# Filter products, butterflies and gate products in fewer, longer VectorE operations, with a new order and a choice of engines

## The chip, the cores and the metric

The kernel runs on one core of a Trainium2 chip. The metric is device time in microseconds: the time of one execution on the device, where the median of several executions is taken. The kernel before takes 239.01 us (three runs, 238.78 to 239.78). The profiled execution has a span of 235.4 us from its first to its last instruction; all times within the kernel are counted from the start of that span.

Five engines matter. TensorE (PE) multiplies matrices, with PEld its weight loads. VectorE (DVE) and ScalarE (ACT) do elementwise work and move results out of PSUM. GpSimd (POOL) issues the loads of q, k, v and the weights, and SyncE (SP) issues the outputs and the transposes by DMA.

## The reference

There are 8 batches, 8 heads, 576 positions and 64 values per head. A linear attention (cosformer) is followed by a gated long convolution (Hyena):

```python
# attention: theta = pi/2 * pos / S
phi(x) = concat(relu(x) * cos(theta), relu(x) * sin(theta))        # 64 -> 128
kv  = einsum('bhsf,bhsd->bhfd', phi(k), v);  z = phi(k).sum(s)
att = einsum('bhsf,bhfd->bhsd', phi(q), kv) / (einsum(phi(q), z) + 1e-6)
x   = att with the heads side by side                               # (8, 576, 512)

# gated convolution
x1, x2, x3 = split(x @ w_proj)                                      # 512 -> 3 * 512
x2_conv = irfft(rfft(x2, axis=1) * rfft(filter, axis=0), n=576)     # along the sequence
out = (x1 * x2_conv * x3) @ w_out
```

## The kernel before

Names in the profile are those of the tiles here. The plan is a list of words: each word runs one more piece of a step (up to its next `yield`), in program order, and every engine takes its own instructions in that order. `'v` behind a word sends an eviction to VectorE instead of ScalarE, `'a` sends a product to ScalarE instead of VectorE, `'b` moves a transposed q in one piece. `~` holds a load back until the last VectorE operation and the last transpose before it in the plan have finished. The first number of a word is the batch; the rest is a channel group, a pair of heads or a part.

```python
def ev(out, in_, mul=None):                  # an eviction: VectorE with 'v, else ScalarE
    ...

def step_pk(b, half):                        # kp: relu(k) * cos, relu(k) * sin
    for j in range(NJ):
        for x, col in enumerate((ccol, scol)):
            if which[0] == "a":
                nc.scalar.activation(out=dst, in_=src, func=AF.Relu, scale=c)
            else:
                tsc(dst, src, c, AL.mult, 0.0, AL.max)
            yield
# step_pq (qp) is alike: relu(q), and relu(q) * tcol for each of five columns
# step_va: v into va, with a column of ones;  step_kv: the matmuls kv<-va,kp
# step_qt: q transposed, on TensorE for batches 0 and 1, by DMA from batch 2 (qpt<-qp)
# step_num: matmuls num<-kvs,qpt, then rcp and att = num * rcp on VectorE
# step_fx: matmuls that fold att along the sequence, and an eviction to fx
# step_xt: att transposed by DMA into xt (batches 1 to 7);  step_xp: on TensorE, batch 0

def step_x2(b, bl):                          # "pr": x2 = fx @ w_proj[x2], evicted to x2f
    ...

def step_dft(b, bl):                         # bl 0, 1: 512 wide; bl 2: 128 wide
    ...                                      # matmuls dft<-x2f,fcos and dft<-x2f,fsin
    yield
    xf = work.tile([128, 2, n], FP16, tag=f"xf{n}", bufs=2)
    ev(xf, u[:, :, 0:n])
    yield
    h = (hE, hO, hL)[bl]
    tt(out=m1, in0=xf, in1=hr, op=AL.mult)
    yield
    tt(out=m2, in0=xf, in1=h[:, 0] broadcast, op=AL.mult)
    yield
    tt(out=yf[:, 0], in0=m1[:, 0], in1=m2[:, 1], op=AL.subtract)
    yield
    tt(out=yf[:, 1], in0=m1[:, 1], in1=m2[:, 0], op=AL.add)
    yield

def step_gate(w):                            # "ga": w = 0 (x1), "gb": w = 2 (x3)
    def gate(b, c):                          # c: one of four groups of 128 channels
        u = unit(f"x{w}_{b}_{c}")
        for i in range(NC):
            for hf in range(2):
                nc.tensor.matmul(u[:, hf, 0:HS], wp16[:, i, ...], xt[:, i, ...], ...)
        yield
        x = work.tile([128, 2, HS], FP16, tag=f"x{w}s", bufs=2)
        ev(x, u[:, :, 0:HS])                 # x0s or x2s
        yield

def step_g(b, c):                            # g = x1 * x3
    tt(out=g[:, c], in0=x0s, in1=x2s, op=AL.mult)
    yield

def step_inv(b, c):                          # six matmuls inv<-itab,yf and inv<-itl,yf
    ...                                      # from all three yf
    yield
    eq = tile([128, 2, 2, QS], FP16, tag="eq", bufs=4)
    ev(eq, u[:, :, 0:HS])
    yield

def step_y(b, c):                            # two levels of butterflies, then the gate
    for x, op in ((0, AL.add), (1, AL.subtract)):
        tt(out=eoh[:, :, :, x], in0=eqt[:, :, 0], in1=eqt[:, :, 1], op=op)
        yield
    tt(out=y[:, c, 0:HS], in0=eo[:, 0], in1=eo[:, 1], op=AL.add)
    yield
    tt(out=y[:, c, HS:S][:, ::-1], in0=eo[:, 0], in1=eo[:, 1], op=AL.subtract)
    yield
    tt(out=ym[:, :, 0:128], in0=ym[:, :, 0:128], in1=g[...], op=AL.mult)
    yield
    tt(out=ye[:, c], in0=ym[:, :, 128:QS], in1=g[...], op=AL.mult)
    yield

# step_out(b, grp): tiles (0,1), (2,3) of y @ w_out, evicted to os (3 buffers);
#   grp 2 is the leftover 64 rows from ye, evicted to os4 (1 buffer)
# step_end(t): the same for the last batch, tile by tile
```

PSUM has four units of two banks (`unit`), which all steps share. The filter's transform is made in the kernel: `step_feo` folds the filter (feo), and `step_h` has the matmuls h_ps and evicts them to hE, hO and hL.

Of the kernel before, what the change touches and what calls it, by code (L numbers as in the profile page):

```python
# [12 lines left out]
FP16 = mybir.dt.float16  # L13
# [4 lines left out]
def kernel(  # L18
# [24 lines left out]
    DM = NH * D  # L43
# [47 lines left out]
    hE = const("hE", [128, 2, DM], FP16)  # L91
    hO = const("hO", [128, 2, DM], FP16)
    hL = const("hL", [128, 3, 128], FP16)
# [379 lines left out]
    def step_h(bl):  # L473
# [3 lines left out]
        if bl < 2:  # L477
            for ci, tab in ((0, hs_), (1, hc)):
                for j in range(3):
                    nc.tensor.matmul(  # L480
                        u[:, ci], tab[:, j, ds(32 + 128 * bl, 128)], feo[:, bl, j],
                        start=(j == 0), stop=(j == 2),
                    )
            yield
            ev((hE, hO)[bl], u, 2.0 / S)
            yield
            return
# [10 lines left out]
        ev(hL.rearrange("p a b -> p (a b)"), u[:, 0, 0:384], wr_col)  # L498
# [39 lines left out]
    def step_va(b, x):  # L538
        hs = slice(2 * x, 2 * x + 2)
        ev(  # L540
            va_buf[b % 2][:, hs, :, 0:D],
            (v32 if b == 0 and x < 2 else raw_t[(b, "v")])[:, hs].rearrange(
                "p h (j d) -> p h j d", j=NJ
            ),
        )
        yield
# [24 lines left out]
    def step_qt(b, hp):  # L571
# [17 lines left out]
        if which[0] == "b":  # L589
            which[0] = ""  # L590
            ev(qpt[:, hsl], u[:, :, 0:SP_])
            yield
            return
# [105 lines left out]
    def step_dft(b, bl):  # L699
# [3 lines left out]
        for comp, tab, c0 in ((0, fcos, 0), (1, fsin, 32)):  # L703
# [7 lines left out]
        xf = work.tile([128, 2, n], FP16, tag=f"xf{n}", bufs=2, name=f"xf{b}_{bl}")  # L711
        ev(xf, u[:, :, 0:n])
        yield
        m1 = work.tile([128, 2, n], FP16, tag=f"m1{n}", bufs=1, name=f"m1_{b}_{bl}")
        h = (hE, hO, hL)[bl]
        hr = h[:, 1].unsqueeze(1).to_broadcast([128, 2, n]) if bl < 2 else h[:, 1:3]
        tt(out=m1, in0=xf, in1=hr, op=AL.mult)
        yield
        m2 = work.tile([128, 2, n], FP16, tag=f"m2{n}", bufs=1, name=f"m2_{b}_{bl}")
        tt(  # L720
            out=m2, in0=xf, in1=h[:, 0].unsqueeze(1).to_broadcast([128, 2, n]), op=AL.mult
        )
        yield
        yf = moe[b]["yf", bl] = work.tile([128, 2, n], FP16, tag=f"yf{bl}", name=f"yf{b}_{bl}")
        tt(out=yf[:, 0], in0=m1[:, 0], in1=m2[:, 1], op=AL.subtract)
        yield
        tt(out=yf[:, 1], in0=m1[:, 1], in1=m2[:, 0], op=AL.add)
        yield

    def step_gate(w):  # L730
        def gate(b, c):
            xt = xt_t[b]
# [6 lines left out]
                    )  # L739
            yield  # L740
            x = work.tile([128, 2, HS], FP16, tag=f"x{w}s", bufs=2, name=f"x{w}s{b}_{c}")
            ev(x, u[:, :, 0:HS])
            moe.setdefault(b, {})["x", w, c] = x.rearrange("p a b -> p (a b)")
# [3 lines left out]
    def step_g(b, c):  # L747
        if "g" not in moe[b]:
            moe[b]["g"] = work.tile([128, NC, S], FP16, tag="g", bufs=2, name=f"g{b}")
        tt(  # L750
            out=moe[b]["g"][:, c], in0=moe[b]["x", 0, c], in1=moe[b]["x", 2, c], op=AL.mult
        )
        yield
# [6 lines left out]
    def step_inv(b, c):  # L760
        yf = [moe[b]["yf", i] for i in range(3)]
        u = unit(f"inv{b}_{c}")
        for comp in range(2):
            for par in range(2):
                nc.tensor.matmul(  # L765
                    u[:, comp, ds(par * QS, QS)], yf[par][:, comp, ds(c * 128, 128)],
# [3 lines left out]
                u[:, comp, 0:HS], yf[2][:, comp], itl[:, c, comp].rearrange("p a b -> p (a b)"),  # L770
# [3 lines left out]
        eq = late["p"].tile([128, 2, 2, QS], FP16, tag="eq", bufs=4, name=f"eq{b}_{c}")  # L774
        ev(eq.rearrange("p a b c -> p a (b c)"), u[:, :, 0:HS])
        moe[b]["eq", c] = eq
        yield

    def step_y(b, c):
        eq = moe[b]["eq", c]  # L780
        eo = late["p"].tile([128, 2, HS], FP16, tag="eo", bufs=2, name=f"eo{b}_{c}")
        eoh = eo.rearrange("p a (t x z) -> p a t x z", t=2, x=2)
        eqt = eq.rearrange("p a b (t z) -> p a b t z", t=2)
        for x, op in ((0, AL.add), (1, AL.subtract)):
            tt(
                out=eoh[:, :, :, x], in0=eqt[:, :, 0], in1=eqt[:, :, 1], op=op
            )
            yield
        if "y" not in moe[b]:
            moe[b]["y"] = late["p"].tile([128, NC, S], FP16, tag="y", bufs=2, name=f"y{b}")  # L790
        y = moe[b]["y"]
        tt(out=y[:, c, 0:HS], in0=eo[:, 0], in1=eo[:, 1], op=AL.add)
        yield
        tt(out=y[:, c, HS:S][:, ::-1], in0=eo[:, 0], in1=eo[:, 1], op=AL.subtract)
        yield
        g = moe[b]["g"]
        ym = y[:, c].rearrange("p (t i) -> p t i", t=4)
        tt(
            out=ym[:, :, 0:128], in0=ym[:, :, 0:128],
            in1=g[:, c, 0:NM].rearrange("p (t n) -> p t n", t=4), op=AL.mult,  # L800
        )
        yield
        if "ye" not in moe[b]:
            moe[b]["ye"] = late["p"].tile([128, NC, 64], FP16, tag="ye", bufs=2, name=f"ye{b}")
        tt(
            out=moe[b]["ye"][:, c].rearrange("p (a t) -> p a t", t=4),
            in0=ym[:, :, 128:QS].rearrange("p t a -> p a t"),
            in1=g[:, c, NM:S].rearrange("p (a t) -> p a t", t=4), op=AL.mult,
# [46 lines left out]
    def step_end(t):  # L855
# [21 lines left out]
        "pr": step_x2, "dft": step_dft, "ga": step_gate(0), "gb": step_gate(2), "g": step_g,  # L877
# [4 lines left out]
    def run(plan, **batch):  # L882
# [27 lines left out]
        ga0.2 gb0.2 pq1.2 ~Lk2.0 ~Lv3.0 g0.1 gb0.3 ga0.3 gb0.3 tf'v fx0.3 pq1.2*2 fx0.3  # L910
        pq1.2*2 ~Lv2.0 pq1.2 qt1.1 ones1 ~Lq3.0 qt1.1'a pk1.2 ~Lq3.1 pq2.2*2 qt1.1'v pq2.2*2
        tf qt1.2 qt1.2'a qt1.2'v qt1.3 qt1.3'a qt1.3'v qt1.0 qt1.0'a qt1.0'v kv1.2*2 tf*2
        feo1 kv1.2 pr0.1 num1.1 tf ti ~Lv2.1 pr0.1 ti*2 num1.0 feo0 num1.0 num1.1*2 pr0.0
        num1.1 num1.2 pr0.0 ~Lo num1.0*2 num1.2*2 h0 ~Lv3.1 pq2.2 dft0.0 ti fx1.1 num1.2
        num1.3 pq2.2 g0.3 h0 h1 fx1.1 num1.3 dft0.0 num1.3*2 xt1 th fx1.2 dft0.0 dft0.1
        dft0.0 pr0.2 h1 fx1.0 fx1.2 dft0.0 fx1.3 dft0.1 h2 pk2.2*2 dft0.0 fx1.0 va2.2'v
        pr0.2 pk2.2 dft0.1 dft0.2 fx1.3 qt2.2 dft0.1 qt2.0 ~Lq4.0 h2 dft0.2*3 ti pr1.2*2
        dft0.2 dft0.1 dft0.2 dft0.1 pr1.0 inv0.0 inv0.1 ti pk2.2 inv0.2 pk2.2 pr1.0 pk2.2
        g0.2 va2.3'v pk2.2 late inv0.0 inv0.3 pq3.2 ga1.0 y0.0*2 inv0.1 pk2.2*2 inv0.2
        inv0.3 va2.0 pq3.2 va2.1 y0.1 y0.0*2 dft1.2 pk2.2 ~Lv4.0 y0.1 y0.2 y0.1 y0.2 y0.0  # L920
        y0.2 y0.1 ~Lk3.0 pr1.1 pq3.2 dft1.2 pq3.2 ga1.0 kv2.2*2 pr1.1 ~Lq4.1 kv2.2 gb1.0
        num2.0 gb1.0 ga1.1 y0.2 y0.3 y0.1 ~Lk4.0 y0.3 ga1.1 num2.0*3 qt2.1 num2.1*2 y0.2
        ~Lk3.1 num2.1 y0.3*2 num2.1 y0.3 dft1.2 dft1.0 dft1.1 pq3.2 gb1.1 dft1.0 num2.2*2
        qt2.3 dft1.1 num2.3 num2.2 num2.3*2 num2.2 num2.3 dft1.0 g1.0 dft1.0 gb1.1 g1.1
        out0.0 dft1.2 fx2.2*2 fx2.1 dft1.2*2 va3.2'v dft1.0 pq3.2 dft1.0 out0.0 out0.1
        va3.3'v dft1.1 fx2.3 y0.2 dft1.1 fx2.1 ga1.2 out0.1 pk3.2 dft1.1*2 fx2.3 xt2 fx2.0
        qt3.0 gb1.2 fx2.0 ga1.3 ga1.2 pr2.2 gb1.2 pk3.2*2 y0.1 pk3.2 va4.1 pr2.2 inv1.0
        ga1.3 ga2.0 pq4.2*2 g1.2 inv1.0 qt3.3 pq4.2 ga2.0 y1.0 inv1.1*2 pk3.2 y1.0 qt3.2
        ~Lq5.0 y1.0 y1.1 ~Lv4.1 y1.1 pr2.1 pk3.2 y1.1*2 y0.3 y1.1 va3.0 inv1.2*2 pr2.1 gb1.3
        y1.0*2 ~Lk4.1 pr2.0 pk3.2 gb1.3 pr2.0 inv1.3 y0.0 y1.2 pk3.2 y1.2*2 pk3.2 inv1.3  # L930
        gb2.0 y1.2*2 y1.3 gb2.0 g1.3 pk3.2 y1.3 out0.2 ~Lk5.0 ~Lk5.1 out0.2 y1.3*3 dft2.0*2
        dft2.2 gb2.1 ga2.1 dft2.2 g2.0 y1.3 dft2.0 va3.1 kv3.2*2 dft2.2 ga2.2 dft2.2 ~Lq5.1
        dft2.0 gb2.1 ga2.1 kv3.2 pq4.2 dft2.0 g2.1 dft2.2 ~Lv5.1 va4.0 ~Lv6.0 qt3.1 num3.0
# [84 lines left out]
```

## Time and profile before

| | |
|---|---|
| time, median of three | 239.01 us |
| span of the profiled execution | 235.4 us |
| TensorE busy, matmuls | 209.4 us, 2276 |
| VectorE busy, instructions | 192.2 us, 656 |
| ScalarE busy, instructions | 168.1 us, 265 |
| GpSimd busy | 66.7 us |
| mean clock granted to TensorE | 0.968 of full |
| moved by DMA | 39.72 MB, 169 GB/s in the mean |

How to read it: busy time is the union of an engine's instructions over the span. A matmul's end is modelled, so a busy TensorE can still lose time to short gaps; the start of the next matmul is firmer than the end of the last. In a group of instructions the mean duration of one holds the whole instruction, of which a part can lie beside the next one on the same engine. "Idle before" names what the engine waited for. The slices are fortieths of the span, with each digit the busy share in tenths. The chain that ended last is the sequence of work that leads, step by step, to the last instruction.

### The profile page before, as it was taken

Reading aid. Unit: us, or ns where it says so; the run is one execution under the profiler, and the core shown is the slowest. Engines: PE = TensorE matmul, PEld = TensorE weight load, DVE = VectorE, ACT = ScalarE, POOL = GpSimd, SP = SyncE. Lnnn points to the kernel's source line nnn. Section 1 sums busy time; section 2 is a strip of 40 time slices with the busy share of each in tenths; the row PEclk is TensorE's granted clock in tenths of the full one; section 3 lists DMA queues with packets and bytes.
Section 4 is the critical chain, followed back from the end, with each engine's and each line's share of the span. In section 5 each row is a group of like instructions: output and inputs, shape, how many; then the busy total and the mean of one; then the engine's idle time right before and its main releaser. Section 6 shows DMA issues by size and latency. Waiting matters only on the chain.

```text
span 235.4 us, 5939 instructions
## 1 busy us (share of the span) xinstructions
PE 209.4 (89%) x2276; PEld 141.4 (60%) x2276; DVE 192.2 (82%) x656; ACT 168.1 (71%) x265; POOL 66.7 (28%) x111
## 2 busy tenths in 40 slices
PE   7097999983999899999899959999999999999880
PEld 2086775452576567675676635766686767667530
DVE  7999897989279889999895947998999696947931
ACT  2579989996377779787777752798876847877711
POOL 8873375800571067400940209100000000000000
PEclk9769999999799999999999997999999999999998
DMA  5999999999999999999999999959945920743053
GB/s 171 191 195 198 189 207 191 159 167 168 181 170 178 205 206 160 183 275 216 164 187 174 167 266 111 219 111 241 234 160 112 191 56 3 162 153 109 5 203 112
DMA packets 96189, 39.72 MB, mean 169 GB/s; under 512 B 64224, under 2 KB 91872, under 8 KB 96160
## 3 DMA queue, kind: packets, MB, share of 16 engines
q0 software_dynamic: 39040, 16.26, 57.0%
q1 hardware_dynamic: 56752, 22.49, 46.2%
q10 hardware_dynamic: 368, 0.59, 0.8%
q8 instruction: 18, 0.29, 0.5%
q14 instruction: 11, 0.09, 0.1%
HBM read 33.69 MB, written 9.44 MB: 183 GB/s over the span
## 4 chain that ended last, share of the span: by engine, by line
PE 52%; DMA 29%; DVE 10%; POOL 3%; ACT 2%; issue 1%; ACTq 0%; SPq 0%; DVEq 0%; POOLq 0%
PE x L736 19%; PE out L816 10%; DMA xt<-att 9%; PE x L678 9%; DMA raw<-in_q_dram 9%; DMA qpt<-qp 6%; DMA filt<-in_moe_filter_fft_dram 4%; PE num L604 3%; DVE att L117 3%; PE kv L561 2%; PE inv L765 2%; PE dft L709 2%; PE inv L769 2%; PE fx L632 2%; PE out L821 1%; DVE kp L112 1%
## 5 line engine op out<-in xcount | busy, mean ns | idle before, releaser
L736 PE MATMUL x<-xt,wp 128*128 128x288 f16 x512 | 69.8, 286 | 5.5 <-DMA xt<-att 4.8
L736 PEld LDWEIGHTS <-wp 128*128 128x128 f16 x512 | 48.4, 98 | 19.9 <-DMA xt<-att 5.3
L678 PE MATMUL x<-wp,fx 128*128 128x512 f16 (+1 forms) x160 | 36.5, 394 | 0.0
L139 ACT ACTIVATE os<-out 128x1024 f32<-128x1024 f32 (+2 forms) x23 | 18.2, 795 | 19.5 <-PE out L816 14.1
L816 PE MATMUL out<-wo,y 128*128 128x512 f16 x128 | 31.7, 393 | 0.0
L139 ACT ACTIVATE x2f<-x 128x1024 f16<-128x1024 f32 (+1 forms) x24 | 21.2, 887 | 10.1 <-PE x L678 10.1
L117 DVE TENSOR_TENSOR att<-num,rcp 128x640 f16<-128x640 f32 x32 | 25.9, 820 | 0.7
L139 ACT CAST x0s<-x 128x576 f16<-128x576 f32 x32 | 20.6, 642 | 6.5 <-PE x L736 3.8
L139 ACT CAST x2s<-x 128x576 f16<-128x576 f32 x32 | 20.6, 644 | 6.3 <-PE x L736 4.0
L117 DVE TENSOR_TENSOR eo<-eq 128x288 f16<-128x288 f16 x64 | 17.6, 303 | 7.0 <-ACT eq L139 6.9
L678 PEld LDWEIGHTS <-fx 128*128 128x128 f16 (+1 forms) x160 | 13.7, 102 | 15.9 <-issue 3.4
L159 POOL DMA_DIRECT2D raw<-in_q_dram x15 | 11.7, 780 | 39.6 <-DMA qpt<-qp 23.3
L139 ACT CAST fx<-fx 128x576 f16<-128x576 f32 x30 | 19.0, 647 | 4.2 <-PE fx L638 3.8
L139 ACT CAST xf<-dft 128x1024 f16<-128x1024 f32 (+1 forms) x24 | 18.3, 810 | 3.7 <-PE dft L709 3.3
L139 ACT CAST eq<-inv 128x576 f16<-128x576 f32 x32 | 19.6, 652 | 1.1 <-PE inv L769 0.9
L816 PEld LDWEIGHTS <-y 128*128 128x128 f16 x128 | 12.3, 100 | 12.8 <-issue 1.8
L159 POOL DMA_DIRECT2D raw<-in_v_dram x14 | 11.1, 793 | 27.9 <-DVE eo L117 14.3
L117 DVE TENSOR_TENSOR g<-x0s,x2s 128x576 f16<-128x576 f16 x32 | 14.5, 452 | 4.9 <-ACT x0s L139 3.0
L117 DVE TENSOR_TENSOR y<-eo 128x288 f16<-128x288 f16 x64 | 17.6, 302 | 0.3
L604 PE MATMUL num<-kvs,qpt 128*128 128x65 f16 x320 | 14.4, 195 | 3.7 <-DMA qpt<-qp 3.3
L604 PEld LDWEIGHTS <-qpt 128*128 128x128 f16 x320 | 12.9, 99 | 7.9 <-DMA qpt<-qp 4.3
L765 PE MATMUL inv<-itab,yf 128*128 128x144 f16 x128 | 17.0, 226 | 0.6 <-DVE yf L117 0.6
(152 smaller groups left out, 398.1 us busy)
## 6 DMA issues: line engine op xcount, KB each, us to landing
out_dram<-os SPq DMA_DIRECT2D x30, 256.0 KB, 3.3
raw<-in_q_dram POOLq DMA_DIRECT2D x14, 256.0 KB, 6.0
raw<-in_k_dram POOLq DMA_DIRECT2D x13, 256.0 KB, 6.4
raw<-in_v_dram POOLq DMA_DIRECT2D x13, 256.0 KB, 6.3
wp<-in_moe_w_proj_dram POOLq DMA_DIRECT2D x3, 512.0 KB, 8.9
out_dram<-os SPq DMA_DIRECT2D x15, 64.0 KB, 3.4
filt<-in_moe_filter_fft_dram POOLq DMA_DIRECT2D x2, 288.0 KB, 9.1
k<-in_k_dram SPq DMA_DIRECT2D x1, 512.0 KB, 4.0
```

What stands on the lines that cost most here:

```text
L117: last_dve[0] = nc.vector.tensor_tensor(out=out, in0=in0, in1=in1, op=op)
L139: return nc.scalar.copy(out=out, in_=in_) if mul is None else nc.scalar.mul(out=out, in_=in_, mul=mul)
L159: first = queue.dma_start(out=rw[:, to, 0 : 4 * D], in_=src[b, hs, 0:NM].rearrange("h (p j) d -> p h (j d)", j=4),)
L561: nc.tensor.matmul(u[:, g, ds((h % 4) * 65, 65)], kp[:, j, h].rearrange("p a b -> p (a b)"), va[:, h, j, 0:65], start=(j == 0), stop=(j == ...
L604: nc.tensor.matmul(u[:, hh, ds(t * 65, 65)], qpt_buf[:, h, ds(t * 128, 128)], kvs[:, h // 4, ds((h % 4) * 65, 65)], start=True, stop=True,)
L632: nc.tensor.matmul(uf[:, ds(256 * t, 144)], att[:, c, t], fm.rearrange("p v a -> p (v a)"), start=(t % 2 == 0), stop=False,)
L678: nc.tensor.matmul(dst, fx[:, c, ds(128 * ch, n)], wp16[:, c, ds(DM, DM)], start=(c == cs[0]), stop=(c == cs[-1]),)
L709: nc.tensor.matmul(u[ds(32 * x, 32), comp, 0:n], st, mv, start=True, stop=True)
L736: nc.tensor.matmul(u[:, hf, 0:HS], wp16[:, i, ds(w * DM + c * 128, 128)], xt[:, i, ds(HS * hf, HS)], start=(i == 0), stop=(i == NC - 1),)
L765: nc.tensor.matmul(u[:, comp, ds(par * QS, QS)], yf[par][:, comp, ds(c * 128, 128)], itab[:, par + 4 * comp], start=(par == 0), stop=False,)
L769: nc.tensor.matmul(u[:, comp, 0:HS], yf[2][:, comp], itl[:, c, comp].rearrange("p a b -> p (a b)"), start=False, stop=True,)
L816: nc.tensor.matmul(dst, y[:, c, ds(QS * t, 128)], wo16[:, c], start=(c == 0), stop=(c == NC - 1),)
```

## The change

It does three things.

1. Fewer and longer operations on VectorE. The three filter tables hE, hO, hL become one table `hm`, and the three DFT results one tile `xf`. The products are four instructions for a batch instead of twelve. The butterflies, their products with the gate and the gate products g work on two channel groups at a time (in the last batch partly still on one). v is copied in pieces of four heads instead of two, except in batch 0.
2. The gate of batch 0 is split: a piece of a gate tile needs only the first two channel groups of xt.
3. The plan is new: another order, other loads first, and other choices of engine for evictions and for the products kp and qp.

```diff
-    hE = const("hE", [128, 2, DM], FP16)
-    hO = const("hO", [128, 2, DM], FP16)
-    hL = const("hL", [128, 3, 128], FP16)
+    NF = 2 * DM + 128
+    hm = const("hm", [128, 3, NF], FP16)
 ...
-            ev((hE, hO)[bl], u, 2.0 / S)
+            ev(hm[:, 0:2, ds(bl * DM, DM)], u, 2.0 / S)
+            yield
+            ev(hm[:, 2, ds(bl * DM, DM)], u[:, 1], 2.0 / S)
             yield
 ...  # step_va
-        hs = slice(2 * x, 2 * x + 2)
+        n = 2 if b == 0 else 4
+        hs = slice(n * x, n * x + n)
 ...  # step_dft: the products leave it
-        xf = work.tile([128, 2, n], FP16, tag=f"xf{n}", bufs=2, name=f"xf{b}_{bl}")
-        ev(xf, u[:, :, 0:n])
-        (m1, m2 and yf for this part: four operations)
+        if "xf" not in moe[b]:
+            moe[b]["xf"] = work.tile([128, 2, NF], FP16, tag="xf", bufs=1, name=f"xf{b}")
+        ev(moe[b]["xf"][:, :, ds(bl * DM, n)], u[:, :, 0:n])
+        yield
+
+    def step_mul(b):
+        xf = moe[b]["xf"]
+        yf = moe[b]["yf"] = work.tile([128, 2, NF], FP16, tag="yf", name=f"yf{b}")
+        tt(out=yf, in0=xf, in1=hm[:, 1:3], op=AL.mult)
+        yield
+        tt(out=xf, in0=xf, in1=hm[:, 0].unsqueeze(1).to_broadcast([128, 2, NF]), op=AL.mult)
+        yield
+        tt(out=yf[:, 0], in0=yf[:, 0], in1=xf[:, 1], op=AL.subtract)
+        yield
+        tt(out=yf[:, 1], in0=yf[:, 1], in1=xf[:, 0], op=AL.add)
         yield
 ...  # step_gate
+                if b == 0 and i == 1:
+                    yield
 ...  # x0s and x2s: tiles of two channel groups, two buffers each
-    def step_g(b, c):
+    def step_g(b, c, n):
+        tt(out=moe[b]["g"][:, c : c + n], in0=x0, in1=x2, op=AL.mult)
 ...  # step_inv: eq is a tile of two channel groups, two buffers instead of four of one
-    def step_y(b, c):
-        eo = late["p"].tile([128, 2, HS], FP16, tag="eo", bufs=2, name=f"eo{b}_{c}")
+    def step_y(b, c, n):
+            moe[b]["eo", c // 2] = late["p"].tile([128, 2, 2, HS], FP16, tag="eo", bufs=1, ...)
 ...  # the six operations of a channel group, each on n groups at once
```

The start of the plan, before and after (it is new throughout):

```diff
-        io0 Sk0.0 cols pad1 ones0 cols pad3 io2 rows Sv0.0 pad2 io1 cols rows cols*2 pad5
-        cols th pad4 cols Lq0.0 cols*2 tf th'v va0.0 rows pk0.0 rows pk0.0'a pk0.0 pk0.0'a
-        rows th'v*2 rows tf rows*2 pk0.0 cols*2 pk0.0'a rows*2 va0.1 Lq0.1 pk0.0 pk0.0'a
-        rows tf pk0.0 pk0.0'a rows Lk0.1 cols Lv0.1 rows cols pad0 Lw2 cols pq0.0 cols*2
-        Lv1.2 pq0.0*5 cols warm0.12 qt0.0 qt0.1 pq0.1 qt0.0'b pq0.1*3 qt0.1'b rows Lw0 pq0.1
 ...
+        pad4 pad5 Sk0.0 pad0 io0 cols pad2 cols io1 cols*2 tf io2 pad1 cols rows cols
+        pk0.0'a th pk0.0'a cols*2 Lq0.0 rows*2 cols pk0.0*2 rows*3 pk0.0 cols*2 pk0.0'a
+        Sv0.0 rows va0.0 pk0.0 va0.1 Lq0.1 rows pk0.0*2 pk0.0'a ones0 cols*2 warm0.12 cols
+        kv0.0 pq0.0 rows pq0.0 pq0.0'a*2 cols Lk0.1 pq0.0'a pq0.0 kv0.0'v pq0.1*2 pq0.1'a
+        pq0.1 pq0.1'a pq0.1 qt0.0 qt0.0'b qt0.3 Lv0.1 pk0.1*3 qt0.1 th'v qt0.3'c va0.2'v
+        rows pk0.1*2 rows pk0.1'a*2 pk0.1 pk0.1'a*2 tf th'v num0.0 qt0.1'b va0.3 cols num0.0
+        qt0.2 kv0.1 num0.0 qt0.2'b num0.1 tf num0.0 xp0.0 num0.1 kv0.1 num0.1*2 num0.2*2
+        rows num0.3 rows xp0.0*2 num0.2 num0.3 num0.2 rows Lw0 xp0.0'a ga0.0 Lk1.2 cols*3
 ...
```

Its end, around the last gate tile and the last outputs:

```diff
-        out6.1 y7.2 out6.1 y7.3 out6.0 y7.2 ga7.3 y7.1 y6.0 y7.1 ga7.3 out6.2 g7.3 out6.2
-        y7.3 end0 y7.3 end0 end1 y7.0 end1 end0'v end1*2 y7.2 out6.1 end4*2 end2*2 out6.2
-        end4'v end3*2 end2'v end0 end4 end2 end3*2
+        y7.2.1 y7.0.2 y7.2.1 out6.0 y7.3.1 y6.2.2 y7.2.1 ga7.3 out6.2 out6.1 ga7.3 y7.2.1
+        out6.2*2 y7.3.1*2 end1 g7.3.1 y7.2.1 y7.3.1 end0*2 end2 end0*2 y7.0.2 end1*2 end2
+        y7.3.1 end4*2 end1 end3 end2'v end2 end4'v end3 end4 end3*2
```

The instructions of VectorE go from 656 to 469; the matmuls stay 2276 and are the same.

## The prediction

> **What bounds the kernel now.** I read the page first (busy shares, then the forty slices).
>
> ```profile
> span 235.4 us, 5939 instructions
> ...
> PE   7097999983999899999899959999999999999880
> DVE  7999897989279889999895947998999696947931
> ACT  2579989996377779787777752798876847877711
> PEclk9769999999799999999999997999999999999998
> DMA  5999999999999999999999999959945920743053
> ```
>
> TensorE is near 9 in most slices; VectorE follows with 192.2 us busy (82%) and ScalarE with 168.1 us (71%). The holes of TensorE are in the first quarter and at the end. For the first 150 us the DMA engines are as full as TensorE. So I cut the span into stretches:
>
> ```profile
> 11.40:38.00 26.60, 24.35 (x319) 20.04 (x320) 24.17 (x87) 22.81 (x38) 14.52 (x20) 0.93 1.42 197
> 38.00:58.50 20.50, 15.47 (x222) 8.85 (x220) 19.07 (x58) 18.52 (x31) 6.83 (x10) 1.00 1.42 167
> 180.00:223.00 43.00, 43.00 (x431) 29.00 (x428) 33.04 (x112) 31.45 (x49) 0.00 (x0) 1.00 0.46 98
> 223.00:228.60 5.60, 4.85 (x33) 2.10 (x32) 2.85 (x10) 1.70 (x4) 0.00 (x0) 1.00 0.61 209
> ```
>
> Columns: stretch, length, then busy time of PE, weight load, DVE, ACT, POOL, then clock. From 180 to 223 us TensorE never rests, though VectorE idles 10 us of 43. The losses are elsewhere: 2.25 us idle before 38, 5.03 before 58.5, 4.4 us in all from 58.5 to 223 (0.99 + 0.66 + 2.77 in 62 to 150), 0.75 in the last matmuls, and 6.8 us after them with no matmul. TensorE's waits say for whom:
>
> ```profile
> PE qt L584 <- DVE qp L112: 6.0, 3, 5.5
> PE x L736 <- DMA xt<-att: 4.8, 2, 3.8
> PE num L604 <- DMA qpt<-qp: 3.3, 2, 2.8
> ```
>
> One is the start; the others are transposes by DMA, not VectorE's filter products or butterflies. The chain that ended last confirms it:
>
> ```profile
> 29.39 8.57 DMA filt<-in_moe_filter_fft_dram
> 38.06 1.82 DVE feo L467 x2
> ...
> 45.47 12.98 DMA xt<-att
> 58.50 1.15 PE x L736 x8
> ```
>
> The filter arrives at 38 us, then the transpose of batch 1 takes 13.0 us where the median is 5.1, behind a backlog of loads.
>
> How much work has TensorE at full rate? From starts of neighbours in the timeline: a gate tile 0.98 us (8 per batch), a 512-wide projection or output pair 1.73 (2+2), a leftover 0.55 (1+1), inverse tile 0.50 (4), fx 0.39 (4), kv 1.27, num 0.31 (4), dft 0.45+0.45+0.13. That is 23.0 us per batch, 184 for eight, and with transposes (4.4+1.1) and filter tables (3.6) 193 us. It runs from 11.4 to 228.5 us, 217 us; the 24 us lost are 12.4 of visible idleness, and the rest clock (mean 0.968) and gaps too short to show.
>
> **What the Trainium skill says.** Four places of the Trainium skill bear on this. (1) Vector Engine (DVE) Microarchitecture Reference, 5.2 Measured stream behaviour on trn2: an instruction costs about 75 ns beyond its elements once queued. The trace agrees:
>
> ```profile
> 107.38 0.30 DVE L117 TENSOR_TENSOR eo<-eq 128x288 f16<-128x288 f16 x1
> 107.60 0.35 DVE L112 TENSOR_SCALAR kp<-raw,ccol 128x512 f16<-128x512 f16 x1
> 107.86 0.35 DVE L112 TENSOR_SCALAR kp<-raw,scol 128x512 f16<-128x512 f16 x1
> ```
>
> A butterfly lasts 0.30 us but the next starts 0.22 later: 0.08 overlaps, and 288 elements at 2 per cycle (0.15 us) leave about 0.07. So merging two instructions saves 0.07 to 0.08 us, not the 0.15 that durations suggest. (2) ScalarE: Activation LUTs, Rules for kernel authors: ReLU and multiplication belong on VectorE. Here a 128x640 fp16 copy takes 741 ns on ScalarE and 329 on VectorE: agrees. (3) VectorE: DVE Perf Modes, The perf-mode tier table: a PSUM operand in fp32 runs at 1x. The fx eviction takes 746 ns on VectorE, 647 on ScalarE: agrees. (4) DMA: Bandwidth & Descriptors, Queues, rings and completion order: an engine round-robins between queues packet by packet, so a transpose shares with the loads; 13.0 against 5.1 us fits.
>
> **The change, part by part.**
>
> *Merging.* Step = duration less 0.08. Filter products per batch: 4 x 0.603 + 2 x 0.206 + 4 x 0.338 + 2 x 0.141 = 4.45 us. The new ones have 2304 and 1152 elements; from 286 ns at 256 and 683 at 1024 the slope is 0.517 ns, so 1345 and 749 ns, and 2 x 1.265 + 2 x 0.669 = 3.87. Saved 0.58 x 8 = 4.7 us. Butterflies: two steps of 0.222 become one like the present 576-wide gate product, 0.372; 60 merges x 0.072 = 4.3. Product with the gate 15 x 0.08, gate product 15 x 0.075, ye 15 x about 0.08: 3.5. Sum 12.5 us of 192.
>
> *Choice of engines.* Counting the new order: 47 scale-and-ReLU products of 512 elements and nine others leave VectorE for ScalarE. VectorE -47 x 0.27 - 3.0 = -15.7; ScalarE +47 x 0.53 (0.64 by the slope of its copies, less 0.11 overlap) + 5.4 = +30.3. In return VectorE takes 23 of the 576-wide evictions (9 x0s, 7 x2s, 4 eq, 3 fx), +23 x 0.67 = 15.4; six xf and six x2f, at 1.02 ns per element from its os evictions (0.425 at 256, 0.686 at 512), 5 x 1.13 + 4 x 0.345 + 3 x 0.606 = 8.8; and nine small ones, about 4.5. ScalarE loses 12.4 + 7.2 + 4.5, and 3.5 on fewer va copies. Sums: VectorE 192 - 12.5 - 15.7 + 28.7, about 193; ScalarE 168 + 30.3 - 27.6, about 171. **What merging frees is spent again**, on evictions that VectorE does slower. TensorE's work stays at 193. So no engine's load falls; what remains is the order.
>
> *Order, start.* The first gate, split, needs only the first half of the channels: it stands after 5.3 us of TensorE work instead of 7.0, and its weights (the x1 third of w_proj) are now the first w_proj load rather than the second, for which the gate waited until 23.4 us. The first kv precedes the transposes, and ScalarE shares the first products, so TensorE's early waits shrink. But the same loads stand before the filter, so 38 us stays, and with it the catching up. Work ahead of batch 1's first gate is 36.2 us instead of 34.4 (x2 projections and DFTs of batch 1 brought forward, two inverse tiles put back). If the transpose still lands near 58, TensorE starts that gate at about 58 instead of 58.5 with 1.8 us more behind it: gain about 2.3.
>
> *Order, middle.* The work between the last num and the first gate of a batch is 9 to 16 us in both kernels, so transposes are covered about as well; the last DFT to the first inverse grows from 8-12 to 10-14 us in batches 2, 4 and 6, which pays for the products now waiting for all three DFTs. Of 4.4 us idle I take back 2.5.
>
> *Order, end.* The end now waits for one single-buffered tile, os4: its eviction in the last batch waits 3.3 us until the output of the batch before has left. That leftover output of batch 6 is issued behind the eviction of the last gate tile today, and TensorE waits 0.72 us for it; in the new order it is issued ahead of that eviction. Gain about 0.8; the buffer stays single.
>
> Sum 2.3 + 2.5 + 0.8 = 5.6, and 239.0 - 5.6 = 233.4 us.
>
> **Rivals.** (a) VectorE was the bound, and merging gives its whole saving, 12.5 us: 226.5. For: 82% busy, early slices full. Against: its long idle time late in the kernel with TensorE at 100%. (b) Coarser steps add waits: products start only when the third DFT is out, xf, yf and eo have one buffer each, a pair of butterflies waits for two inverse tiles, and ScalarE's slower ReLUs delay kp and qp. One more microsecond per batch would make 241. For: the short cover in batch 0 (4.5 us of TensorE work for 3.87 of products, an xf eviction of 0.35 and a va copy of 0.41). Against: the longer covers elsewhere. (c) Loads bind the first 58 us and all is hidden: only middle and end count, 236. For: full DMA slices.
>
> **Range and chances.** The best case removes 12.4 us of idleness and some of the late start, 226 to 227; new waits of 5 us cancel the gain. I take 227.5 to 238.5. Two percent lies at 234.2, just above my value: faster 0.58, same 0.34, slower 0.08.
>
> **What would show it.** Right: VectorE busy 185 to 196 us and ScalarE 165 to 175 despite 187 fewer VectorE instructions; TensorE's wait for the first qp gone; filter still at 38 us; batch 1's first gate at 56 to 58.5; 1 to 3 us idle in the middle; os4 still awaited at the end. Wrong: batch 1's gate below 54 us (loads not binding), VectorE below 180 (merging worth more), or TensorE idle more than 5 us between 60 and 220.

## The result and the profile after

The changed kernel takes 231.20 us (median of four, 228.09 to 231.84); the kernel before, beside it, 238.89 us (237.31 to 239.78). The ratio is 0.964, with a 95% interval of 0.953 to 0.976. Predicted were 233.4 us and a range of 227.5 to 238.5. Ratios here leave out executions more than 1.5% above the fastest of their kernel (of the 55 of before beside e1 to e4 that is 30, at 235.5 to 240.4 us, while the others lie at 231.9 to 235.3), so they are not always the quotient of the medians.

The kernel before is the less steady of the two. Beside the experiments, on two chips, its medians were 235.9, 235.7 and 234.2 us; the changed kernel, measured again on the first of them, took 231.23 us, which is a ratio of 0.987 (0.983 to 0.990). The direction is firm. The size is 1.3% to 3.6%, depending on where before is measured: in the first measurement all four of its executions were above 237 us. Why before moves that much was not found.

The page of the profile after has the span, the busy times and the slices:

```profile
span 229.9 us, 5779 instructions
...
PE 209.2 (91%) x2276; PEld 141.7 (62%) x2276; DVE 195.5 (85%) x469; ACT 172.0 (75%) x271; POOL 63.7 (28%) x105
...
PE   6496998999999899977999999999799999999990
...
PEclk9769999999999999995899999999999999999997
DMA  5999999999999999999999999999769833831074
```

187 fewer instructions, and VectorE is busier than before (195.5 against 192.2 us): the freed time was spent on other work. In the first quarter of TensorE the slices of 0 and 3 tenths have become 4 and 9. There are new holes in the middle, and beside the first of them the granted clock falls to 5 tenths. The stretches (columns as in the prediction; the last three are clock, DMA share and GB/s):

```profile
11.40:38.00 26.60, 23.40 (x294) 18.65 (x292) 23.21 (x82) 22.11 (x38) 13.47 (x18) 0.93 1.43 198
38.00:58.50 20.50, 18.96 (x252) 10.28 (x251) 19.99 (x42) 19.17 (x33) 4.79 (x7) 1.00 1.41 194
...
90.00:120.00 30.00, 26.64 (x288) 17.89 (x287) 20.49 (x45) 22.10 (x33) 10.92 (x16) 0.89 1.40 173
...
180.00:210.00 30.00, 30.00 (x290) 19.61 (x289) 24.11 (x42) 16.89 (x26) 0.00 (x0) 1.00 0.46 129
```

From 38 to 58.5 us TensorE idles 1.54 us instead of 5.03. From 90 to 120 it now idles 3.36. TensorE's waits, the longest by name (total, times, longest):

```profile
PE x L736 <- DMA xt<-att: 4.0, 2, 3.4
PE kv L563 <- DVE ph L111: 2.4, 1, 2.4
...
PE num L606 <- ACT os L138: 1.3, 1, 1.3
```

The 5.5 us for the first qp and the 2.8 us for a transposed q are gone. What is left is again a transpose of att. It was batch 1's; it is now batch 3's, as the chain that ended last shows (start, duration, what):

```profile
94.10 11.01 DMA xt<-att
105.15 2.10 PE x L736 x8
107.25 2.04 PE dft L711 x24
```

In the profiled executions the spans are 235.4 and 229.9 us, 5.5 apart. The medians are 7.7 apart: the profiled execution of before took 237.16 us, less than its median, and that of the changed kernel 231.84, the longest of its four. The 5.5 us divide as follows. Batch 1's first gate starts at 57.38 us instead of 58.50, and by the prediction's count 1.8 us more work lies behind it: 2.9. From the end of the last gate tile (219.36 instead of 222.99) to the end of the span it is 10.5 us instead of 12.4: 1.9. The remaining 0.7 is the middle.

### The profile page after: what moved, and what is told of

Its sections match the earlier page's. It is cut to its first block, busy times and chain, and to the rows that moved or that the text cites. A ratio compares the mean times of both kernels' runs of the same rounds, so it can differ in the third digit from the quotient of the medians.

```text
span 229.9 us, 5779 instructions
## 1 busy us (share of the span) xinstructions
PE 209.2 (91%) x2276; PEld 141.7 (62%) x2276; DVE 195.5 (85%) x469; ACT 172.0 (75%) x271; POOL 63.7 (28%) x105
## 4 chain that ended last, share of the span: by engine, by line
PE 54%; DMA 24%; DVE 11%; POOL 3%; issue 3%; ACT 2%; SPq 1%; DVEq 0%; POOLq 0%; ACTq 0%
PE x L736 19%; DMA raw<-in_q_dram 10%; PE out L824 9%; DMA xt<-att 8%; PE x L680 8%; DMA out_dram<-os 4%; PE dft L711 3%; PE num L606 3%; PE kv L563 2%; PE inv L770 2%; PE inv L774 2%; DMA raw<-in_k_dram 2%; PE fx L634 2%; DVE kp L111 2%; PE out L829 1%
## 5 line engine op out<-in xcount | busy, mean ns | idle before, releaser
L736 PE MATMUL x<-xt,wp 128*128 128x288 f16 x512 | 72.2, 288 | 5.7 <-DMA xt<-att 4.0
L138 ACT ACTIVATE os<-out 128x1024 f32<-128x1024 f32 (+2 forms) x22 | 16.8, 761 | 16.3 <-PE out L824 10.6
L158 POOL DMA_DIRECT2D raw<-in_q_dram x14 | 11.0, 786 | 59.5 <-ACT x0s L138 13.8
L138 ACT ACTIVATE x2f<-x 128x1024 f16<-128x1024 f32 (+1 forms) x18 | 16.0, 905 | 9.9 <-PE x L680 9.9
L138 ACT CAST x0s<-x 128x576 f16<-128x576 f32 x23 | 14.9, 649 | 9.5 <-PE x L736 9.1
L138 ACT CAST x2s<-x 128x576 f16<-128x576 f32 x25 | 16.3, 654 | 4.0 <-PE x L736 3.8
L138 ACT CAST eq<-inv 128x576 f16<-128x576 f32 x28 | 17.2, 653 | 2.5 <-PE inv L774 2.5
L774 PE MATMUL inv<-itl,yf 128*128 128x288 f16 x64 | 16.6, 286 | 0.0
L116 DVE TENSOR_TENSOR eo<-eq 128x576 f16<-128x576 f16 (+1 forms) x34 | 14.1, 432 | 2.7 <-ACT eq L138 2.4
L563 PE MATMUL kv<-va,kp 128*128 128x65 f16 x320 | 12.9, 196 | 3.4 <-DVE ph L111 2.4
L138 ACT CAST xf<-dft 128x1024 f16<-128x1024 f32 (+1 forms) x18 | 14.8, 879 | 1.3 <-PE dft L711 0.7
L532 ACT ACTIVATE qp<-raw,tcol 128x512 f16<-128x512 f16 (+1 forms) x23 | 15.2, 693 | 0.0
## 6 DMA issues: line engine op xcount, KB each, us to landing
raw<-in_v_dram POOLq DMA_DIRECT2D x2, 512.0 KB, 12.3
```

Of the source, the lines that this page charges most:

```text
L116: last_dve[0] = nc.vector.tensor_tensor(out=out, in0=in0, in1=in1, op=op)
L138: return nc.scalar.copy(out=out, in_=in_) if mul is None else nc.scalar.mul(out=out, in_=in_, mul=mul)
L158: first = queue.dma_start(out=rw[:, to, 0 : 4 * D], in_=src[b, hs, 0:NM].rearrange("h (p j) d -> p h (j d)", j=4),)
L532: nc.scalar.activation(out=t[:, hs, j, 1], in_=rj[:, :, j], func=AF.Relu, scale=tcol[:, j : j + 1])
L563: nc.tensor.matmul(u[:, g, ds((h % 4) * 65, 65)], kp[:, j, h].rearrange("p a b -> p (a b)"), va[:, h, j, 0:65], start=(j == 0), stop=(j == ...
L736: nc.tensor.matmul(u[:, hf, 0:HS], wp16[:, i, ds(w * DM + c * 128, 128)], xt[:, i, ds(HS * hf, HS)], start=(i == 0), stop=(i == NC - 1),)
```

## The experiments

Kernels e1 to e8 ran on one chip, in two groups of four (before: 235.9 and 235.7 us), e9 to e12 on another (before: 234.2 us). All changes are to the changed kernel unless it says otherwise.

| kernel | median us (lowest to highest) | ratio to before |
|---|---|---|
| e1, merged operations taken apart | 232.08 (230.07 to 233.69) | 0.988 (0.977 to 0.998) |
| e2, before's plan with merged operations | 235.45 (234.12 to 239.72) | 1.009 (1.006 to 1.012) |
| e3, choice of engines undone | 233.89 (232.75 to 236.35) | 0.998 (0.995 to 1.000) |
| e4, the changed kernel again | 231.23 (228.24 to 235.95) | 0.987 (0.983 to 0.990) |
| e5, batch 3 transposed on TensorE | 232.32 (231.77 to 233.88) | 0.986 (0.977 to 0.995) |
| e6, matmuls in the wait | 231.44 (228.68 to 233.50) | 0.979 (0.968 to 0.990) |
| e7, two os buffers shared at the end | 232.50 (230.54 to 234.91) | 0.982 (0.970 to 0.994) |
| e8, e5 and e7 | 232.83 (230.08 to 235.50) | 0.991 (0.987 to 0.995) |
| e9, two loads moved | 229.33 (227.89 to 230.30) | 0.981 (0.975 to 0.987) |
| e10, e7 and a second os4 buffer | 229.86 (227.89 to 231.32) | 0.981 (0.973 to 0.989) |
| e11, e9, e10 and an output moved | 230.87 (229.87 to 232.85) | 0.989 (0.980 to 0.998) |
| e12, batch 0's gate whole | 230.52 (228.88 to 231.72) | 0.986 (0.979 to 0.993) |

e2, e3, e4 and e8 were executed 20 times each, the others four times. Landmarks from the profiled execution of each, in us:

| kernel | batch 1's first gate | batch 3's transpose: issued, landed | last gate tile ends | from there to the end |
|---|---|---|---|---|
| changed | 57.4 | 94.1, 105.1 | 219.4 | 10.5 |
| e4 (the same) | 57.2 | 93.8, 104.9 | 220.6 | 10.1 |
| e1 | 59.7 | 97.2, 105.5 | 221.6 | 10.3 |
| e3 | 59.4 | 96.3, 104.0 | 221.3 | 10.9 |
| e7 | 57.4 | 93.8, 104.5 | 220.0 | 11.1 |
| e9 | 57.0 | 93.8, 100.6 | 217.6 | 10.4 |
| e10 | 56.9 | 93.5, 103.6 | 219.9 | 9.6 |
| e11 | 56.9 | 92.9, 100.0 | 219.6 | 9.6 |
| e12 | 59.3 | 95.4, 102.6 | 218.1 | 10.3 |

**Which part gave the gain: e1 to e4.** The theory was that the order gives it and merging nothing; the rival, that VectorE's instruction count was the bound.

e1 takes the merged operations apart in the new order:

```diff
-        tt(out=yf, in0=xf, in1=hm[:, 1:3], op=AL.mult)
+        for r in (slice(0, DM), slice(DM, 2 * DM), slice(2 * DM, NF)):
+            tt(out=yf[:, :, r], in0=xf[:, :, r], in1=hm[:, 1:3, r], op=AL.mult)
 ...  # likewise the other three products, the butterflies and the gate products: per channel group
```

> The changed kernel with its order and engines kept, but every merged operation taken apart again into its old pieces, back to back (products in three parts, butterflies and gate products one channel group at a time). Theory 'order': the gain comes from the order; VectorE gets 10 to 13 us more busy time (about 206), but most of it lies beside other work: 231.5 to 234 us. Rival 'merging': VectorE's freed time is the gain: 237 to 243 us.

e2 keeps before's order and choice of engines, and merges within it:

```diff
 ...  # the changed kernel's steps, batch 0's gate whole, va in before's pieces
-        (the new plan)
+        (before's plan; mul{b} stands where the last products of its DFTs stood, and
+         g and y of a pair of channel groups where the later one of the two stood)
```

> The kernel before in its own order and with its own engines, but with the merged operations, each put where the last of its old pieces stood. Theory 'order': VectorE 178 to 182 us busy, time within 2 us of the kernel before (237 to 240), because TensorE's waits for the transposes are as they were. Rival 'merging': 227 to 231 us.

e3 undoes the letters that choose engines, from batch 1 on:

```diff
-        ... pk1.2'a pk1.2 ... pq1.2'a ... gb0.3'v ... ga5.0'v ... inv2.0'v ... dft2.2'v
+        ... pk1.2 pk1.2 ... pq1.2 ... gb0.3'v ... ga5.0 ... inv2.0 ... dft2.2
```

> The changed kernel with the choice of engines undone from batch 1 on for the products kp and qp (all on VectorE) and for the evictions of gates, inverse, fx, DFT and projections (all on ScalarE); the order of TensorE is the same. Theory 'order with engines': the order was laid out for the choice, so PSUM units come free later: VectorE about 185 us, ScalarE about 167, time 232.5 to 237. Rival 'the choice only spends what merging frees': 231 us or less.

> The changed kernel again, on the same chip as the runs beside it, so that they can be compared with it: 229 to 232 us.

Measured: e1 takes 232.08 us with VectorE busy 204.9 us in 638 instructions, against 231.23 (e4) with 195.8 in 469. Nine microseconds less of VectorE are worth 0.85 us by the medians, and the ratios are 0.988 and 0.987; the interval of e1, with four executions, leaves 1% either way open. In before's order (e2) VectorE falls from 192.2 to 181.5 us and nothing is won: the ratio is 1.009. TensorE's waits in e2:

```profile
PE qt L586 <- DVE qp L111: 6.0, 3, 5.5
PE inv L768 <- DVE yf L116: 4.9, 7, 2.1
PE x L736 <- DMA xt<-att: 2.6, 1, 2.6
```

The first and third line are before's own. The second is new: the inverse waits 4.9 us for products that now start only after all three DFTs. Before, that wait came to 0.6 us. The plan of the change leaves no such wait; there is none in its profile. So merging needs the new order, and by itself it buys nothing here.

e3's plan differs from e2's in order, in batch 0 (the split gate and the new plan's choices there), in the pieces of v, and in choices for other work that e3 keeps (v, transposed q, kv, outputs): e2's plan has before's 42 letters for an engine, e3's 52, the changed kernel's 131. From e4 it differs only in the choice, 79 letters. From e2 to e3 the ratio falls from 1.009 to 0.998 and the median by 1.6 us, from e3 to e4 to 0.987 and by 2.7 us; the intervals of the ratios do not overlap in either step. So the choice of engines, in this order, is worth about 1.1%, and the order, with what goes with it, 0.7% to 1.1%. Without the choice the merged kernel in the new order (e3) was not shown to be faster than before. The choice costs VectorE and ScalarE 8.6 and 10.6 us more of busy time (195.8 and 171.8 against 187.2 and 161.2), and yet the kernel is faster. e3's waits of TensorE show a part of why:

```profile
PE kv L563 <- DVE ph L111: 2.5, 1, 2.5
PE x L680 <- ACT fx L138: 2.2, 3, 1.3
```

The first line is in the changed kernel too (2.4 us). The second, fx evictions on a ScalarE that had other work ahead of them, is 0.5 us there. Batch 1's first gate is 2.1 us later in e3 than in e4, and the num matmuls that start at 158.64 us in e4 start at 162.45 in e3. In the profiled execution of e4, one of its longer ones (232.43 us), the wait and low clock at 162 to 168 us, shown below, then took nearly all of that back.

**Does the start's gain reach the end: e12.** The gate of batch 0 is made whole again:

```diff
-                if b == 0 and i == 1:
-                    yield
 ...  # and the first of the words ga0.x and gb0.x of each group leaves the plan
```

> The changed kernel with batch 0's gate not split by channel halves (the second half of the gate's work again waits for all of the transposed input). Theory (the order, not the split, gives the start's gain, because the start is bound by transfers): within 1 us of 231.2, and batch 1's first gate within 1 us of 57.4. Rival (the split fills TensorE in the start): TensorE waits 1 to 2 us more before 58 us, 232.5 to 234.

Each side is right in half. TensorE loses 2 us at the start: the first gate matmul moves from 19.8 to 22.6 us, batch 1's first gate from 57.4 to 59.3. The time, 230.52 us, shows none of it; but the intervals of the ratios (0.979 to 0.993, and 0.983 to 0.990 for e4) would hide a loss of 1.5 us, and the changed kernel itself was not run on that chip. TensorE's longest wait from 60 to 130 us in e12:

```profile
PE num L606 <- DMA qpt<-qp: 2.0, 1, 2.0
```

The wait for batch 3's transpose, 3.4 us in the changed kernel, is gone: its transpose is issued 1.3 us later and lands 2.5 us earlier. e1 and e3 are the same kind: 2 us behind at 58 us, no wait over 0.3 us for that transpose. With the loads in their place it lands at 102.6 to 105.5 us in all of them, whether issued at 93.5 or 97.2. A start that is 2 us better is spent there.

**What that transpose waits for: e5, e6, e9.** Theory: loads fill the DMA queues until some 150 us, and what is awaited depends on their order. Rival of e5: the transpose alone is the fault.

e5 moves batch 3's transpose to TensorE:

```diff
-        ... fx3.1 num3.3 ... xt3 fx3.2 ...
+        ... inv2.0'v xp3.0*2 xp3.0'v*2 ... pr3.2 xp3.1*2 xp3.1'v*2 ...
```

> The changed kernel, but att of batch 3 is transposed on TensorE (20 matmuls, 1.1 us, and four evictions on VectorE) instead of by DMA. Theory 'transpose behind loads, and the clock': the wait of 3.2 to 3.4 us before batch 3's first gate goes, and with it the halved clock after it where the profile had that: 1.5 to 4 us faster than the changed kernel (231.2 in the last runs), 227 to 230 us. Rival: another wait (a PSUM unit, kv or q of batch 4) takes its place at once: 230.5 to 232.5.

It gains nothing, 232.32 us. The chain that ended last in e5:

```profile
91.72 0.74 POOL raw L158
92.46 13.81 DMA raw<-in_v_dram
...
106.35 1.26 ACT va L138
107.61 0.93 ACT x2f L138
...
108.58 2.36 PE kv L563 x40
```

The transposes of batch 4's q, which had followed xt3 on SyncE from 99.1 us on, now start at 87.4 us; a V load issued at 91.7 takes 13.8 us, and TensorE waits 6.9 us for kv. One transfer less, and another is late.

e6 puts 14 matmuls that nobody reads into the wait, so that TensorE is not idle:

```diff
+    def step_fill(i, n):
+        u = unit(f"fill{i}")
+        for x in range(n):
+            nc.tensor.matmul(u[:, x % 2], ident, wo16[:, x % NC], start=True, stop=True)
+        yield
 ...
-        ... inv2.2'v pr3.0 ga3.0 pr3.1 ...
+        ... inv2.2'v pr3.0 fill0.14 ga3.0 pr3.1 ...
```

> The changed kernel, with 14 matmuls of 128x128x512 that nothing reads (3.0 us at full rate) put in front of batch 3's first gate, where TensorE waits for the transpose. Theory 'an idle TensorE loses its clock for some us': the wait stays about as long but the clock stays at full there in every run, so the slow half of the runs goes: median 0.5 to 2 us below the changed kernel, and a narrower spread. Rival 'the clock falls for another reason': no gain, or up to 1 us slower, for the matmuls may push the gate back.

What it is about is seen in the changed kernel's stretches around the wait:

```profile
103.00:105.00 2.00, 0.00 (x0) 0.00 (x0) 0.00 (x0) 0.00 (x0) 0.00 (x0) 0.78 1.43 188
105.00:107.00 2.00, 1.85 (x8) 1.04 (x8) 0.00 (x0) 0.00 (x0) 0.00 (x0) 0.50 1.28 275
...
109.00:111.00 2.00, 2.00 (x18) 1.00 (x15) 0.94 (x3) 1.42 (x2) 1.84 (x3) 0.52 1.12 223
111.00:113.00 2.00, 2.00 (x22) 1.28 (x21) 0.66 (x3) 0.73 (x1) 2.00 (x4) 1.00 1.09 128
```

After 3.4 us of idleness TensorE runs at half clock for 6 us; the gate's eight matmuls take 2.10 us instead of 1.15. In e6 the same stretch is at full clock:

```profile
103.00:105.00 2.00, 2.00 (x13) 1.03 (x12) 0.00 (x0) 0.00 (x0) 0.00 (x0) 1.00 1.19 237
105.00:107.00 2.00, 2.00 (x39) 0.98 (x38) 1.19 (x4) 1.59 (x3) 0.00 (x0) 1.00 1.50 117
```

But so it is in e4, e7 and e10, without these matmuls and with waits of 2.2 to 3.2 us there, so this alone shows nothing. A later wait of 2.3 us for an os eviction, at 161 us, was followed by a low clock in e6, and the median, 231.44, is not below 231.23: the gain was not shown. In e4, the same kernel again, the 3.2 us wait for that transpose left the clock at 1.00, and a wait of 2.9 us that ended at 165 was followed by a low one:

```profile
103.00:105.00 2.00, 0.06 (x1) 0.06 (x2) 0.00 (x0) 0.00 (x0) 0.00 (x0) 1.00 1.38 180
...
164.00:166.00 2.00, 0.94 (x18) 0.94 (x18) 0.17 (x1) 2.00 (x3) 0.00 (x0) 0.64 0.04 14
166.00:168.00 2.00, 2.00 (x14) 1.29 (x12) 1.83 (x5) 0.08 (x1) 0.00 (x0) 0.51 0.00 0
```

Which wait is hit differs between executions of the same kernel. The two also show what the low clock cost. At 94 us they are 0.03 us apart, and both wait until 105. The same num matmuls after that, in the changed kernel and in e4:

```profile
116.39 0.47 PE L606 MATMUL num<-kvs,qpt 128*128 128x65 f16 x10
114.08 0.47 PE L606 MATMUL num<-kvs,qpt 128*128 128x65 f16 x10
```

That is 2.3 us, of which 0.2 is the later landing.

e9 changes only where two loads stand, in the order of GpSimd, which issues them (not of SyncE, as my expectation has it):

```diff
-        ... pk3.2 ~Lq5.1 pq4.2 ... out0.1 ~Lv4.0 gb2.2*2 ~Lv5.1 num3.1 ... pr3.0 ga3.0 pr3.1 ...
+        ... pk3.2 ~Lv4.0 ~Lq5.1 pq4.2 ... out0.1 gb2.2*2 num3.1 ... pr3.0 ga3.0 ~Lv5.1 pr3.1 ...
```

> The changed kernel with two loads in another place of SyncE's order: the first half of V of batch 4 is issued ahead of the second half of Q of batch 5 (it is wanted long before that), and the second half of V of batch 5 only after batch 3's first gate. Theory (the transfers bind up to some 150 us, and which one is awaited depends on the order of the loads): fewer loads lie beside batch 3's transpose, it lands within 8 us instead of 11.0, the wait of 3.4 us of batch 3's first gate and the low clock after it go, 228 to 230 us. Rival (the sum of the bytes binds, the order only picks the victim): another load or transpose is awaited for 2 us or more between 85 and 130 us, within 1 us of the changed kernel's 231.2.

The transpose of batch 3 in e4, and in e9, issued at the same 93.8 us:

```profile
L660 SPq DMA_TRANSPOSE xt<-att x1: 4747/4747/4747, 93.8 to 93.8; - x1
...
DMA to landing us min/median/max: 11.1/11.1/11.1
```

```profile
L660 SPq DMA_TRANSPOSE xt<-att x1: 4771/4771/4771, 93.8 to 93.8; - x1
...
DMA to landing us min/median/max: 6.8/6.8/6.8
```

6.8 us instead of 11.1. The Trainium skill says in DMA: Bandwidth & Descriptors, Queues, rings and completion order, that an engine takes a packet from each queue in turn; that a transfer then lands later the more else is queued is my conclusion, and it agrees. One change of the loads' place moved the landing by 4.3 us. In five executions with the loads in the old place (the changed kernel, e4, e6, e7, e10), issued at 93.5 to 94.1 us, it took 10.1 to 11.1 us; in the two with them moved (e9, e11) 6.8 and 7.1. TensorE then idles 0.84 us from 90 to 120 us, at clock 1.00. The kernel's median is 229.33 us, as expected, but its interval (0.975 to 0.987) overlaps that of e4 (0.983 to 0.990), on another chip: that it is faster than the changed kernel was not shown.

**The end: e7, e8, e10.** In the changed kernel's last 15 us ScalarE waits for a buffer:

```profile
ACT os L138 <- DMA out_dram<-os: 2.4, 1, 2.4
```

e7 lets two end tiles share one os buffer, so that the ring of three suffices; e8 has e5's edit too:

```diff
-        os_ = late["p"].tile([128, 2, DM], FP32, tag="os", bufs=3, name=f"os{b}_{t}")
-        ev(os_[:, 0], u[:, 0], OUTSC)
+        if ("end", t // 2) not in late:
+            late["end", t // 2] = late["p"].tile([128, 2, DM], FP32, tag="os", bufs=3, name=f"os{b}_{t}")
+        os_ = late["end", t // 2][:, t % 2]
+        ev(os_, u[:, 0], OUTSC)
```

> The changed kernel, with the last batch's four tiles in two os buffers (two tiles share one, in its two halves) instead of one buffer each out of three, so that the last eviction doesn't wait for the first tile's output to leave. Theory 'the end waits for an os buffer': the wait of 2.4 us goes, 1.5 to 2.5 us faster than the changed kernel. Rival 'the last outputs wait for DMA anyway': within 0.5 us of it.

> TensorE's transpose for batch 3 and the shared buffers at the end together. The two lie far apart on the path, so by both theories their gains add: 3 to 6.5 us faster than the changed kernel, 225 to 228 us. Rival: 230 us or more.

In e7 VectorE waits in place of the ring, for os4:

```profile
DVE os L111 <- DMA out_dram<-os: 1.6, 1, 1.6
```

That is the buffer which the prediction had named. ScalarE's last eviction still comes 3.0 us late, since an issue of that tile's output stands ahead of it on ScalarE (which issues some of the last outputs) and waits for VectorE's eviction. The stretch from the last gate tile to the end is 11.1 us, not shorter, and the time, 232.50 us, is not lower. In e8 os4 was not awaited and the stretch was 9.7 us, but e5's wait for kv was there again, 7.6 us, and the time was 232.83 us.

e10 gives os4 a second buffer on top of e7:

```diff
-        os_ = late["p"].tile([128, DM // 2], FP32, tag="os4", bufs=1, name=f"os{b}_4")
+        os_ = late["p"].tile([128, DM // 2], FP32, tag="os4", bufs=2, name=f"os{b}_4")
```

> The changed kernel with the end tiles sharing two buffers of the os ring, and two buffers for the last tile's os4 instead of one: both waits of the end's evictions for outputs on their way are taken away. Theory (buffers bind the last 10.5 us): last gate tile to end 8 to 9 us, 229 to 230 us. Rival (the output transfers themselves bind, all leave through the same queues in the last microseconds): last gate tile to end stays at 10 us or more, within 1 us of 231.2.

The longest waits from 217 to 230 us in e10:

```profile
ACT os L138 <- PE out L824: 4.2, 5, 1.4
DVE os L111 <- PE out L824: 1.1, 1, 1.1
```

No output is awaited any more; the evictions wait for matmuls alone. The stretch is 9.6 us in e10 and in e11, against 10.5 and 10.1 in the changed kernel: 0.5 to 0.9 us, where I expected 1.5 to 2.5; and as e7 and e8, whose ends are alike, differ by 1.4 us, even this is not firm. The time is 229.86 us, with an interval of the ratio that overlaps that of e4. From the start of the last eviction, at 225.0 us, it is still 4.5 us to the end of the span; that part was not touched.

**All together: e11.** e9 and e10, and the issue of batch 2's first output pair follows its eviction instead of standing behind xt5 and four transposes:

```diff
-        ... out2.0 out1.0 num5.0 ... xt5 ... qt6.3 ... num6.0 out3.1 out2.0 out3.1 ...
+        ... out2.0 out1.0 out2.0 num5.0 ... xt5 ... qt6.3 ... num6.0 out3.1 out3.1 ...
```

> The load order of e9_load_order, the end of e10_end_both, and batch 2's first output pair leaves SyncE right after its eviction instead of after batch 5's transpose and four transposes of batch 6 (19 us later in the changed kernel). Theory: the three waits add up, 225 to 228.5 us, faster than both kernels. Rival (each wait gives its place to another): 230 to 232.

The three waits it aims at are gone, and the time is 230.87 us: the rival is right. Its longest wait is now

```profile
PE x L736 <- DMA xt<-att: 4.4, 2, 4.2
```

for batch 4's transpose, issued at 113.0 us and landed after 12.3. At its issue e11 is 6.2 us ahead of the changed kernel (119.2) and 4.0 ahead of e4 (117.0). At that of batch 5's, at 145.9 us, it is 0.6 ahead of the one (146.5) and 2.0 behind the other (143.9). The same load order gave a wait of 1.3 us for the same transpose in e9.

No version was shown to beat the changed kernel.

## Why the prediction was right or wrong

**Direction and size.** Faster was right. The time was 2.2 us below the point value, within the range. In the profiled executions the difference is 5.5 us, where the sum of the steps was 5.6; but that agreement is luck. All three terms were off: start and end by 0.6 and 1.1 us too small, the middle by 1.8 too large. And it holds for the two executions that were profiled, not for the medians.

**Merging.** Right in kind: it frees VectorE and moves the time hardly at all. The durations were well worked out. Groups of the changed kernel, mean ns behind the busy time:

```profile
L116 DVE TENSOR_TENSOR eo<-eq 128x576 f16<-128x576 f16 x30 | 13.0, 449 | 2.6 <-ACT eq L138 2.4
...
L514 ACT ACTIVATE kp<-raw,ccol 128x512 f16<-128x512 f16 x16 | 11.7, 730 | 0.0
L116 DVE TENSOR_TENSOR yf<-yf,xf 128x1152 f16<-128x1152 f16 x16 | 11.6, 753 | 0.2
...
L116 DVE TENSOR_TENSOR yf<-xf,hm 128x2304 f16<-128x2304 f16 x8 | 10.8, 1351 | 0.5 <-ACT xf L138 0.5
```

1351 and 753 ns stand against 1345 and 749, and the merged butterfly, 449 ns or a step of 0.37, against 0.372. The sum of 12.5 us was too large: e2 has 10.7 less than before, e1 9.1 more than e4. Where the other 2 to 3 us are was not traced. Rival (a), that VectorE is the bound and merging gives 12.5 us of time, falls with e1 and e2. Rival (b), that coarser products add waits, is true in the old order (4.9 us in e2) and not in the new.

**Choice of engines.** The sums were close: VectorE 195.5 for 193, ScalarE 172.0 for 171, though its scaled ReLU takes 0.73 us and not 0.64 (0.34 to 0.36 on VectorE). The step failed in what it concluded from them. "So no engine's load falls; what remains is the order" counted loads, and gave the choice no term of its own; e3 shows it to be worth 1.1%, with both loads higher. That is nearly all of the 1.3% by which the changed kernel beats before on that chip; what remains without it, merging and order, is level with before (0.998). That what counts is which engine is free when a result is wanted fits the waits for fx (2.2 us to 0.5); no run moved one eviction alone.

**Start.** The mechanism was right: the filter lands at 38.1 us as before, the wait for the first qp is gone (6.0 us to 0.2), and batch 1's gate starts at 57.38 us, in the predicted 56 to 58.5. The term, 2.3, measured 2.9 at that point. What failed is that I carried it into the sum in full. e12 gives up 2 us of it and was not shown to be slower. The premise "loads bind the first 58 us" belonged to rival (c), and it should have been drawn out to 150 us. Until there the DMA share, taken over stretches of 20 to 30 us, is 1.20 or more in both profiles; the last of them, before and changed:

```profile
120.00:150.00 30.00, 27.23 (x278) 17.66 (x277) 22.39 (x73) 18.03 (x28) 8.80 (x13) 0.94 1.20 181
120.00:150.00 30.00, 30.00 (x343) 20.51 (x341) 28.35 (x59) 25.61 (x39) 8.18 (x12) 1.00 1.20 191
```

**Middle.** Wrong. "The work between the last num and the first gate of a batch is 9 to 16 us in both kernels, so transposes are covered about as well" took a transpose's duration as given. TensorE idles 5.3 us from 58.5 to 220, which I had named as a sign of being wrong above 5, and the half clock after the 3.4 us wait cost some 2 us more (by comparison with e4). The idle of 4.4 us did not shrink by 2.5. The middle is 0.7 us better net. The transpose of batch 3 landed after 11.0 us behind loads, and e9 and e11 show that their place was the cause (6.8 and 7.1 with two of them moved).

**End.** Right in sign, too small: 0.8 predicted, 1.9 measured. TensorE's wait of 0.72 us before the leftover output is gone, as predicted. That os4 is "still awaited at the end" did not come true. The ring of os, with three buffers, was awaited in its place, 2.4 us where os4 had cost 3.3; os4 was next in line (e7).

**What stays open.** Why before varies between 234 and 239 us from one measurement to the next; where, beside the fx evictions, the choice of engines gains its 1.1%; and which load order would keep the transposes of batches 3 and 4 both early.

## What to carry to other kernels

Where transfers are queued for most of the kernel, a better start is a loan: check at the next awaited transfer whether it landed earlier too, before adding the gain to the sum. Merging operations on an engine that is seldom awaited bought nothing here, and can cost waits if the order is not changed with it; of an eviction, ask which engine is free at that moment, not whose total is lower. When a wait is removed and the time stands still, look for the wait that took its place (xt3, then a V load, then xt4; os, then os4) before removing the next.

## What the runs showed of the hardware that was not expected

A wait of some 3 us can cost TensorE more than its length. In the changed kernel a clock of 0.50 followed the 3.4 us for 6 us, which cost 2 us more; in the kernel before it was 0.69 and then 0.50 from 59 to 63 us, after its wait of 3.8. The Trainium skill, TensorE: Matmul & The Clock Gate, Part 1: The HAM clock gate, gives half rate after an idle window of about 3.4 us that runs freely, so that it depends on the phase. The second half fits: in one execution (e4) a wait of 3.2 us left the clock at 1.00 and one of 2.9 us lowered it. The length does not quite: in e6 a wait of 2.3 us was followed by 0.58 and 0.57 over the 4 us from 164.

A transpose of att by DMA took anything from 4.8 to 14.3 us to land (both in e2). Batch 3's, behind the same loads, landed at 102.6 to 105.5 us whenever it was issued: after 10.1 to 11.1 us from 93.5 to 94.1, after 7.2 to 8.3 from 95.4 to 97.2.
